# Weight conversion, start-up work and planner settings changed in a fused linear-attention and MLP kernel

## The chip, the core and the metric

The kernel runs on one core of a Trainium2 chip. The core has a matrix engine (PE, TensorE; its weight loads are shown as PEld), a vector engine (DVE, VectorE), an activation engine (ACT, ScalarE), a general engine (POOL, GpSimd) and a queue engine (SP, SyncE), each with an instruction stream of its own that runs in order; they wait for each other by semaphores. DMA transfers between HBM and on-chip memory are issued by SP, and by ACT where the program says so. Products go to PSUM, everything else lies in SBUF; POOL can't reach PSUM. The metric is the device time of one execution in microseconds (us).

## The reference

```python
def phi(x):                                   # q, k, v: (8, 8, 576, 64); w_phi: (64, 128)
    proj = np.einsum('bhsd,df->bhsf', x, w_phi)
    proj = proj - np.max(np.abs(proj), axis=-1, keepdims=True)
    return np.concatenate([np.exp(proj), np.exp(-proj)], axis=-1)
q_p, k_p = phi(q), phi(k)
kv = np.einsum('bhsf,bhsd->bhfd', k_p, v)
z = np.sum(k_p, axis=2)
num = np.einsum('bhsf,bhfd->bhsd', q_p, kv)
den = np.einsum('bhsf,bhf->bhs', q_p, z)[..., None] + 1e-06
x = (num / den), as (8 * 576, 512)            # heads side by side
h = x @ w_in                                  # w_in (512, 2048), float64
g = h * (1.0 / (1.0 + np.exp(-1.702 * h)))
out = (g @ w_out).astype(np.float32)          # w_out (2048, 512), float64
```

The two weight matrices of the last part arrive as 64-bit floats.

## The kernel before

Accuracy is kept by splitting numbers in two 16-bit halves (a high part and what is left of it, names that end in `h` and `l`): each product of two such numbers is three products of halves. The work has two kinds.

*Attention*, batch by batch, in pairs of heads (`attention_first` for the first batch, mostly in 32-bit products; `attention` for the others). Per pair: load k, q and v (`attn_load`: tiles `kt`, `qt`, `vn`), split and turn them (`turned`: `xs`, then a transposing DMA to `xT`), project (`ab` or `at` in PSUM), subtract the maximum (`sm`, `t` on DVE), exponentials on ACT (`e`), split those (`eh` a cast, `el` a subtraction), then products with the values (`kf`, `kz`) and of queries with them (`n`, `nf`), a division (`rc`, `xf`) and the way back to columns (`xo`, `x`). The last 64 rows of all heads of a batch, the tail, are loaded by `tail_load` (tile `tl`, six DMAs) and go through `attn_tail`. The kernel's first product needs the first batch's tail.

*The MLP*, in chunks of 256 or 384 rows (`moe_chunk`): for each of 16 blocks of 128 hidden columns, products into `hb`, tanh (`th`, ACT), `g` (DVE), split into `gh` (ACT) and `gl` (DVE), and products into `ab`.

*The weights* (`load_weights`, 32 blocks of 128 x 512): a block is loaded as 64-bit numbers into `raw`. Each number is two 32-bit words, low and high. ACT copies the high word, taken as a 32-bit float, with a scale into `y` (a PSUM bank `hb` for the first 16 blocks, the SBUF tile `wy` for the others). Two scalings in place, each on any of three engines, work on 16-bit pieces: one brings the top 16 bits of the low word into the high word's low half, one leaves the sign alone in its upper half. Then DVE shifts `y` left by 3 bits and ORs the high word in. The result is split into `w16` (a cast and a subtraction, both shown as `w`). Some 16-bit pieces lie 8 bytes apart.

*The order* is not that of the program text. A `Recorder` notes each operation with the engines that may run it (`three`: DVE, ACT or POOL; `two`: DVE or POOL; `evac`: ACT or DVE), and `schedule` plans the whole program as a list: it keeps a time at which each engine is free, a cost for every operation by engine (`cost`), a delay from each engine to those that use its result (`_READY`), and takes the candidate that can start first; among those that can start at once, the one of the lowest priority number. Priorities come from a place on an axis given to each part of the program (`PLACES`, one pair for each `part`). An operation that may run on several engines is put on one only if no other would finish it earlier by the planner's count, where the cost on each engine is multiplied by `price`. `emit` (line 460) then issues the instructions in that order, so all recorded instructions bear the line L460 in the profile and are told apart by tile names. `wmx`, maxima of the weights, is planned after 250 us.

Ahead of the recorded program stand constants: an identity (`ident`, `ii`), `ones`, and memsets of padding in `vn`, `vs`, `vts`, `zt` and of the two rows of limits `low` and `high`, all on POOL except `ii`.

Of the kernel before, what the change touches and what calls it, by code (L numbers as in the profile page):

```python
# [99 lines left out]
class _Op:  # L100
# [34 lines left out]
_READY = {"tensor": 282.5, "scalar": 240.0, "vector": 305.0, "gpsimd": 300.0, "sync": 100.0}  # L135
# [41 lines left out]
class Recorder:  # L177
    price = dict(tensor=1.000, scalar=0.514, vector=1.148, gpsimd=1.165, sync=1.000)
# [25 lines left out]
    def record(self, alts, also):  # L204
        o = _Op()
        o.eng, o.meth, o.args, o.kw = alts[0]
        o.alts = []
        for e, m, a, k in alts:
            assert e != "gpsimd" or not any(
                isinstance(x, V) and "PSUM" in str(x.t.space) for x in a  # L210
            )
            c = self.cost(e, m, a, k)
            if e == "tensor":
                o.load, o.cost, o.passes = c
            o.alts.append((e, m, c[1] if e == "tensor" else c, self.shared(e, m, a), a, k))
        if o.eng != "tensor":
            o.load, o.cost, o.passes = 0.0, o.alts[0][2], 1
        o.deps, o.outs, o.allocs, o.uses = {}, [], [], []
        o.left, o.end, o.est, o.after = 0, None, 0.0, self.after
        args, kw = o.args, o.kw  # L220
        views = [(args[0], True)]
        views += [(a, False) for a in args[1:]]
        views += [(a, n == "accum_out") for n, a in kw.items()]
        for a, write in views:
            if not isinstance(a, V):
                continue
            self.touch(o, a, write)
        for a in also:
            self.claim(o, a.tl)
        o.left = len(o.deps)  # L230
        for d in o.deps:
            d.outs.append(o)
        self.group.append(o)
        o.prio = o.eng in self.first
        self.ops.append(o)
# [96 lines left out]
    def schedule(self):  # L332
# [15 lines left out]
        free = {"tensor": 0.0, "scalar": 0.0, "vector": 1900.0, "gpsimd": 6200.0, "sync": 700.0}  # L348
# [4 lines left out]
        def ready(o):  # L353
            est = o.after
            for d, data in o.deps.items():
                if data:
                    lat = _READY[d.eng]
                    if d.meth.startswith("dma"):
                        lat = _READY["sync"]
                    elif d.eng == o.eng:  # L360
                        lat = 115.0 if d.eng in ("vector", "scalar") else 0.0
# [9 lines left out]
        while todo:  # L371
            best = None
            for e, c in cand.items():
                t = free[e]
                pick = None
                for o, alt in c:
                    s = max(t, o.est, turn + o.load) if e == "tensor" else max(t, o.est)
                    ok = True
                    for a in o.alts:
                        w = max(free[a[0]], o.est) + a[2] * self.price[a[0]]  # L380
# [31 lines left out]
            if alt[3] and o.eng in ("vector", "gpsimd"):  # L412
                s = max(s, port - 70.0)
                port = s + o.cost
# [6 lines left out]
            if o.meth.startswith("dma"):  # L421
                free[o.eng] = s + (650.0 if o.eng == "sync" else 800.0)
# [44 lines left out]
def attn_moe_fast(ctx, tc, q, k, v, w_phi, w_in, w_out, out):  # L467
# [88 lines left out]
    nc.gpsimd.memset(ones, 1.0)  # L556

    NQ = B + 4
    low, high = (cp.tile([1, NQ], F32, name=n) for n in ("low", "high"))
# [3 lines left out]
    for i, (a, b) in enumerate(lo_hi):  # L563
        nc.gpsimd.memset(low[:, i : i + 1], a)
        nc.gpsimd.memset(high[:, i : i + 1], b)

    for ap in pools["vn"].aps:
        nc.gpsimd.memset(ap[:, :, D : D + 1], ONE)
        nc.gpsimd.memset(ap[:, :, D + 1 : DV], 0.0)
    for ap in pools["vs"].aps:  # L570
        nc.gpsimd.memset(ap, 0.0)
        nc.gpsimd.memset(ap[:, :, 0, D : D + 1], ONE)
    for ap in pools["vts"].aps:
        nc.gpsimd.memset(ap, 0.0)
        for a in range(2):
            nc.gpsimd.memset(ap[a * D : a * D + D, :, a, 0, D : D + 1], ONE)
    for ap in pools["zt"].aps:
        nc.gpsimd.memset(ap, 0.0)
# [34 lines left out]
    def load_weights(j, bank):  # L613
        js = slice(j * P, (j + 1) * P)
        for i, src in (
# [7 lines left out]
            else:  # L623
# [3 lines left out]
                hi = raw.bitcast(I32).rearrange("p (n w) -> p n w", w=2)[:, :, 1]  # L627
                r16 = raw.bitcast(U16).rearrange("p (n w) -> p n w", w=4)
# [3 lines left out]
                R.three.scale(r16[:, :, 2], r16[:, :, 1], 0.9375 * 2.0**-13)  # L632
                R.three.scale(r16[:, :, 3].bitcast(F16), r16[:, :, 3].bitcast(I16), 2.0**-60)
                R.vector.scalar_tensor_tensor(
                    y.bitcast(I32), y.bitcast(I32), 3, hi, ALU.logical_shift_left, ALU.bitwise_or
# [19 lines left out]
    def attn_load(b, hp):  # L655
        kt, qt, vn = new("kt"), new("qt"), new("vn")
        for t, src in ((kt, k), (qt, q)):
            R.sync.dma_start(
# [3 lines left out]
        for a in range(2):  # L662
            R.sync.dma_start(
# [5 lines left out]
    def tail_load(b):  # L669

        t = new("tl")
        for i, src in enumerate((k, q, v)):
            for a in range(2):
                R.sync.dma_start(
# [374 lines left out]
    def in_range():  # L1049


        s = small(16, "sc")
# [143 lines left out]
    def attention_first():  # L1196
# [8 lines left out]
        nat = [attn_load(0, 0)]  # L1205
        tl = tail_load(0)
# [236 lines left out]
```

## Time and profile before

| what | value |
|---|---|
| median of 3 runs | 1100.02 us (1097.91 to 1100.56) |
| the profiled execution, its own time | 1100.22 us |
| its span, first to last instruction | 1098.5 us |
| mean granted TensorE clock | 0.986 of full speed |
| DMA | 181020 packets, 80.93 MB, mean 74 GB/s; HBM read 45.15 MB, written 9.44 MB |
| chain that ended last, by engine | PE 60%, DVE 23%, ACT 8%, the rest 9% |
| largest PE groups | into `hb`: 3264 products, 452.4 us; `gh` into `ab`: 1152, 319.3 us; `gl` into `ab`: 576, 189.5 us |
| weight loads | 32 DMAs of 512 KB, 3.8 us from issue to landing |
| tail loads | 48 DMAs of 64 KB, 2.5 to 2.7 us from issue to landing |

How to read the profile's lines: a group names the line, the engine, the operation, the tile written and the tiles read, the shapes, the count, then busy us and mean ns of one, then the idle time of the engine just before them and what ended it. A row of the view by stretches of time gives the stretch and its length, busy us (and count) of PE, PEld, DVE, ACT and POOL, the granted TensorE clock, the busy share of the DMA engines and GB/s. The timeline gives start, duration, engine, line, operation and tiles. Busy time of PE contains a modelled drain, so products of one group overlap. SPq and ACTq are the DMA issues of SP and ACT.

### The profile page before, as it was taken

The numbers are of one execution on the slowest core, as the hardware profiler recorded it, in microseconds if no ns is written. First come the engines' busy times: TensorE is split into PE (matmuls) and PEld (weight loads), VectorE is DVE, ScalarE is ACT, GpSimd is POOL, SyncE is SP. The second block draws the span as 40 slices with busy tenths as digits, with TensorE's granted clock in tenths as the row PEclk, the third lists the DMA queues.
The fourth block names the chain that finished last, engine by engine and source line by source line (L and its number), as shares of the span: only waits on it lengthen the run. The fifth ranks groups of instructions, "written<-read, shape, count | busy, mean of one in ns | idle before, by whom it ended". The sixth has DMA issues, their size and how long they took to land.

```text
span 1098.5 us, 24641 instructions
## 1 busy us (share of the span) xinstructions
PE 1022.5 (93%) x9874; PEld 671.3 (61%) x9874; DVE 808.4 (74%) x1506; ACT 629.6 (57%) x1357; POOL 354.2 (32%) x461
## 2 busy tenths in 40 slices
PE   4877888999999999999999999999999999999996
PEld 3544556667765666567776555667766655577553
DVE  4888898989999989998899423787887776323232
ACT  4898889667547676665676322655464554232221
POOL 3105764355525535555545000222343211000000
PEclk9987999999999999999999999999999999999998
DMA  7656463253434334323535101132131120000101
GB/s 193 183 172 172 112 143 96 72 112 84 54 73 86 90 90 97 81 69 88 93 78 109 32 1 39 49 87 50 43 75 39 30 48 12 1 30 1 29 1 33
DMA packets 181020, 80.93 MB, mean 74 GB/s; under 512 B 149536, under 2 KB 174240, under 8 KB 180896
## 3 DMA queue, kind: packets, MB, share of 16 engines
q1 hardware_dynamic: 180736, 79.00, 30.4%
q8 instruction: 79, 1.29, 0.5%
q14 instruction: 45, 0.37, 0.1%
q10 hardware_dynamic: 160, 0.26, 0.1%
HBM read 45.15 MB, written 9.44 MB: 50 GB/s over the span
## 4 chain that ended last, share of the span: by engine, by line
PE 60%; DVE 23%; ACT 8%; issue 3%; DMA 3%; SPq 1%; POOL 1%; DVEq 0%; ACTq 0%; POOLq 0%
PE ab L460 25%; PE hb L460 24%; PE at L460 11%; DVE el L460 4%; DVE gl L460 3%; ACT raw L460 2%; DVE sm L460 2%; DVE g L460 2%; DVE t L460 2%; ACT e L460 2%; DVE wmx L460 1%; DMA xT<-xs 1%; SPq L460 1%; DVE xf L460 1%; DVE mq L460 1%
## 5 line engine op out<-in xcount | busy, mean ns | idle before, releaser
L460 PE MATMUL hb<-x,w 128*128 128x192 f16 (+3 forms) x3264 | 452.4, 280 | 2.5 <-DVE g L460 1.6
L460 PEld LDWEIGHTS <-w 128*128 128x128 f16 x3264 | 279.5, 98 | 108.3 <-issue 6.1
L460 PE MATMUL ab<-w,gh 128*128 128x512 f16 x1152 | 319.3, 380 | 4.3 <-ACT gh L460 2.2
L460 DVE SCALAR_TENSOR_TENSOR g<-th,hb 128x384 f32<-128x384 f32 (+1 forms) x208 | 107.2, 517 | 148.7 <-ACT th L460 148.1
L460 ACT ACTIVATE th<-hb 128x384 f32<-128x384 f32 (+1 forms) x208 | 96.8, 467 | 198.4 <-PE hb L460 191.8
L460 PE MATMUL ab<-w,gl 128*128 128x512 f16 x576 | 189.5, 380 | 5.2 <-DVE gl L460 4.9
L460 PEld LDWEIGHTS <-gh 128*128 128x128 f16 x1152 | 107.0, 98 | 103.2 <-ACT gh L460 5.6
L460 DVE SCALAR_TENSOR_TENSOR gl<-g,gh 128x384 f16<-128x384 f32 (+1 forms) x208 | 135.7, 654 | 38.1 <-ACT gh L460 37.8
L460 ACT ACTIVATE gh<-g 128x384 f16<-128x384 f32 (+1 forms) x208 | 103.5, 499 | 80.8 <-DVE g L460 79.1
L460 DVE TENSOR_TENSOR el<-e,eh 128x512 f16<-128x512 f32 x161 | 134.0, 846 | 6.2 <-PE at L460 2.2
L460 PEld LDWEIGHTS <-eh 128*128 128x128 f16 x1856 | 111.4, 97 | 30.3 <-issue 5.5
L460 POOL TENSOR_TENSOR el<-e,eh 128x512 f16<-128x512 f32 x71 | 95.1, 1344 | 74.9 <-DVE eh L460 32.5
L460 PEld LDWEIGHTS <-el 128*128 128x128 f16 x928 | 86.1, 98 | 26.0 <-DVE el L460 16.3
L460 PE MATMUL at<-ph,xT 128*128 128x128 f16 x1008 | 91.6, 219 | 4.3 <-DVE t L460 1.5
L460 PEld LDWEIGHTS <-gl 128*128 128x128 f16 x576 | 53.9, 98 | 65.2 <-DVE gl L460 14.5
L460 PEld LDWEIGHTS <-xT 128*128 128x128 f16 x1056 | 73.7, 99 | 32.6 <-DMA xT<-xs 15.5
L460 ACT CAST eh<-e 128x512 f16<-128x512 f32 x145 | 87.8, 619 | 6.6 <-PE at L460 5.7
L460 POOL TENSOR_TENSOR n<-n,cs 128x132 f32<-128x132 f32 (+1 forms) x75 | 45.6, 610 | 136.4 <-ACT n L460 83.3
L460 ACT ACTIVATE e<-t 128x512 f32<-128x512 f32 x128 | 75.9, 626 | 22.7 <-DVE t L460 21.0
L460 ACT ACTIVATE e<-at 128x512 f32<-128x512 f32 x136 | 76.6, 601 | 14.4 <-PE at L460 12.0
L460 PE MATMUL at<-kz,eh 128*128 128x66 f16 x960 | 78.4, 194 | 4.3 <-DVE nf L460 1.4
L460 PE MATMUL at<-vs,eh 128*128 128x66 f16 x896 | 70.2, 194 | 1.5 <-DVE vs L460 0.6
(187 smaller groups left out, 1396.2 us busy)
## 6 DMA issues: line engine op xcount, KB each, us to landing
kt<-in_k_dram SPq DMA_DIRECT2D x32, 256.0 KB, 2.9
qt<-in_q_dram SPq DMA_DIRECT2D x32, 256.0 KB, 3.0
vn<-in_v_dram SPq DMA_DIRECT2D x64, 128.0 KB, 2.9
raw<-in_moe_w_in_dram SPq DMA_DIRECT2D x16, 512.0 KB, 3.8
raw<-in_moe_w_out_dram SPq DMA_DIRECT2D x16, 512.0 KB, 3.8
out_dram<-e SPq DMA_DIRECT2D x38, 128.0 KB, 2.4
out_dram<-e SPq DMA_DIRECT2D x16, 256.0 KB, 2.4
xT<-xs SPq DMA_TRANSPOSE x68, 2.8
```

Of the source, the lines that this page charges most:

```text
L460: f(*[g(a) for a in o.args], **{k: g(a) for k, a in o.kw.items()})
```

## The change

Five things change together.

1. *Weights.* The scaling that isolates the sign goes. In its place DVE takes the larger of `y` and the high word times -(2^-79): for a positive weight that is `y`, for a negative one a positive number 2^32 times as large, whose higher exponent becomes the sign bit after the shift by 3. The remaining scaling reads the top 16 bits of the low word and writes its result as a 32-bit integer over the whole low word, and the OR takes that word in place of the high one.
2. *Ones.* 40 products of `ones` with itself are issued first on PE, into the first `hb` bank.
3. *Memsets.* The padding of `vn`, `vs`, `vts` and `zt` moves from POOL to DVE; the limits `low` and `high` are set where they are used, in `in_range`, as recorded POOL operations.
4. *Loads.* The first batch's six tail DMAs, and the two V DMAs of its first pair, are issued by ACT; the tail is recorded ahead of the pair.
5. *Planner.* All of `PLACES` but the MLP's own chunks, `_READY`, `price` and the engines' first free times have new values; an issuing engine is now held for a DMA by its size (510 to 660 ns by bytes, 1350 for a transposing one, where it was 650 or 800); the delay within an engine is 125 ns on all but PE (before 115 on DVE and ACT, 0 on POOL); and the port that DVE and POOL share is looked at when a candidate is weighed, not only after it was taken.

```diff
-_READY = {"tensor": 282.5, "scalar": 240.0, "vector": 305.0, "gpsimd": 300.0, "sync": 100.0}
+_READY = {"tensor": 215.0, "scalar": 150.0, "vector": 130.0, "gpsimd": 95.0, "sync": 100.0}
...
-    price = dict(tensor=1.000, scalar=0.514, vector=1.148, gpsimd=1.165, sync=1.000)
+    price = dict(tensor=1.000, scalar=0.004, vector=2.234, gpsimd=1.174, sync=1.000)
...
+            if o.meth == "dma_start_transpose":
+                o.load = 1350.0
+            elif o.meth.startswith("dma"):
+                o.load = 660.0 if o.cost < 900.0 else 510.0 if o.cost < 1800.0 else 440.0
...
-        free = {"tensor": 0.0, "scalar": 0.0, "vector": 1900.0, "gpsimd": 6200.0, "sync": 700.0}
+        free = {"tensor": 5700.0, "scalar": 700.0, "vector": 3400.0, "gpsimd": 1500.0, "sync": 700.0}
...
-                        lat = 115.0 if d.eng in ("vector", "scalar") else 0.0
+                        lat = 0.0 if d.eng == "tensor" else 125.0
...
+                    if alt[3]:
+                        s = max(s, port - 70.0)
...
-                        w = max(free[a[0]], o.est) + a[2] * self.price[a[0]]
+                        w = max(free[a[0]], o.est, port - 70.0 if a[3] else 0.0)
+                        w += a[2] * self.price[a[0]]
...
-                free[o.eng] = s + (650.0 if o.eng == "sync" else 800.0)
+                free[o.eng] = s + o.load
...
+    for i in range(40):
+        nc.tensor.matmul(hb.aps[0][:, 0:P], ones, ones, start=True, stop=True)
...
-        nc.gpsimd.memset(ap[:, :, D : D + 1], ONE)
-        nc.gpsimd.memset(ap[:, :, D + 1 : DV], 0.0)
+        nc.vector.memset(ap[:, :, D : D + 1], ONE)
+        nc.vector.memset(ap[:, :, D + 1 : DV], 0.0)
...
-                hi = raw.bitcast(I32).rearrange("p (n w) -> p n w", w=2)[:, :, 1]
-                r16 = raw.bitcast(U16).rearrange("p (n w) -> p n w", w=4)
+                r32 = raw.bitcast(I32).rearrange("p (n w) -> p n w", w=2)
+                lo, hi = r32[:, :, 0], r32[:, :, 1]


                 R.scalar.activation(y, hi.bitcast(F32), AF.Copy, scale=2.0**-111)
-                R.three.scale(r16[:, :, 2], r16[:, :, 1], 0.9375 * 2.0**-13)
-                R.three.scale(r16[:, :, 3].bitcast(F16), r16[:, :, 3].bitcast(I16), 2.0**-60)
                 R.vector.scalar_tensor_tensor(
-                    y.bitcast(I32), y.bitcast(I32), 3, hi, ALU.logical_shift_left, ALU.bitwise_or
+                    y, hi.bitcast(F32), -(2.0**-79), y, ALU.mult, ALU.max
+                )
+                top = raw.bitcast(U16).rearrange("p (n w) -> p n w", w=4)[:, :, 1]
+                R.three.scale(lo, top, 0.9375 * 2.0**-13)
+                R.vector.scalar_tensor_tensor(
+                    y.bitcast(I32), y.bitcast(I32), 3, lo, ALU.logical_shift_left, ALU.bitwise_or
                 )
...
-    def attn_load(b, hp):
+    def attn_load(b, hp, dk=R.sync, dq=R.sync, dv=R.sync):
...
-    def tail_load(b):
+    def tail_load(b, queue=R.sync):
...
+        for i, (a, b) in enumerate(lo_hi):
+            R.gpsimd.memset(low[:, i : i + 1], a)
+            R.gpsimd.memset(high[:, i : i + 1], b)
...
-        nat = [attn_load(0, 0)]
-        tl = tail_load(0)
+        tl = tail_load(0, R.scalar)
+        nat = [attn_load(0, 0, dv=R.scalar)]
```

The lines of `PLACES`, some 90 pairs of new numbers, are left out here.

More of the change, by code (lines that the diff above doesn't have):

```diff
@@ L411, in schedule @@
                 o.cost = alt[2]
-            if alt[3] and o.eng in ("vector", "gpsimd"):
-                s = max(s, port - 70.0)
+            if alt[3]:
                 port = s + o.cost
@@ L556, in attn_moe_fast @@
     nc.gpsimd.memset(ones, 1.0)
+    for i in range(40):
+        nc.tensor.matmul(hb.aps[0][:, 0:P], ones, ones, start=True, stop=True)
     NQ = B + 4
-    low, high = (cp.tile([1, NQ], F32, name=n) for n in ("low", "high"))
+    low, high = (static(n, [1, NQ], F32) for n in ("low", "high"))
     lo_hi = [(2.0**-6, 2.0)] * B + [
@@ L562, in attn_moe_fast @@
     ]
-    for i, (a, b) in enumerate(lo_hi):
-        nc.gpsimd.memset(low[:, i : i + 1], a)
-        nc.gpsimd.memset(high[:, i : i + 1], b)
     for ap in pools["vn"].aps:
-        nc.gpsimd.memset(ap[:, :, D : D + 1], ONE)
-        nc.gpsimd.memset(ap[:, :, D + 1 : DV], 0.0)
+        nc.vector.memset(ap[:, :, D : D + 1], ONE)
+        nc.vector.memset(ap[:, :, D + 1 : DV], 0.0)
     for ap in pools["vs"].aps:
-        nc.gpsimd.memset(ap, 0.0)
-        nc.gpsimd.memset(ap[:, :, 0, D : D + 1], ONE)
+        nc.vector.memset(ap, 0.0)
+        nc.vector.memset(ap[:, :, 0, D : D + 1], ONE)
     for ap in pools["vts"].aps:
-        nc.gpsimd.memset(ap, 0.0)
+        nc.vector.memset(ap, 0.0)
         for a in range(2):
-            nc.gpsimd.memset(ap[a * D : a * D + D, :, a, 0, D : D + 1], ONE)
+            nc.vector.memset(ap[a * D : a * D + D, :, a, 0, D : D + 1], ONE)
     for ap in pools["zt"].aps:
-        nc.gpsimd.memset(ap, 0.0)
+        nc.vector.memset(ap, 0.0)
     vmx = static("vmx", [P, B], F32)
@@ L652, in w2 @@
         return w16[:, 2 * j + 1, part]
-    def attn_load(b, hp):
+    def attn_load(b, hp, dk=R.sync, dq=R.sync, dv=R.sync):
         kt, qt, vn = new("kt"), new("qt"), new("vn")
-        for t, src in ((kt, k), (qt, q)):
-            R.sync.dma_start(
+        for t, src, queue in ((kt, k, dk), (qt, q, dq)):
+            queue.dma_start(
                 t.rearrange("p (a j) d -> p a (j d)", a=2),
@@ L662, in attn_load @@
         for a in range(2):
-            R.sync.dma_start(
+            dv.dma_start(
                 vn[:, 4 * a : 4 * a + 4, 0:D],
@@ L673, in tail_load @@
             for a in range(2):
-                R.sync.dma_start(
+                queue.dma_start(
                     t[D * a : D * a + D, i],
```

42 rows, old and new, of the table PLACES are left out of this document.

## The prediction

> **What bounds the kernel now.** I read the page first, then its busy times by stretch of the span.
>
> ```profile
> span 1098.5 us, 24641 instructions
> PE 1022.5 (93%) x9874; PEld 671.3 (61%) x9874; DVE 808.4 (74%) x1506; ACT 629.6 (57%) x1357; POOL 354.2 (32%) x461
> ```
>
> ```profile
> core 0: us, PE busy (x) PEld busy (x) DVE busy (x) ACT busy (x) POOL busy (x), PEclk, DMA share, GB/s
> 0.00:15.00 15.00, 0.06 (x1) 0.06 (x2) 2.73 (x8) 4.19 (x7) 5.82 (x47) 1.00 0.74 190
> 15.00:200.00 185.00, 149.88 (x1274) 103.37 (x1275) 160.60 (x289) 161.39 (x316) 78.59 (x92) 0.94 0.54 146
> 200.00:600.00 400.00, 386.47 (x4636) 267.45 (x4635) 376.27 (x685) 263.50 (x608) 198.99 (x237) 1.00 0.40 85
> 600.00:1050.00 450.00, 446.76 (x3758) 280.14 (x3756) 255.40 (x499) 189.77 (x407) 70.84 (x86) 1.00 0.15 36
> 1050.00:1098.50 48.50, 39.31 (x211) 20.30 (x209) 13.35 (x27) 10.73 (x21) 0.00 (x0) 0.94 0.06 19
> ```
>
> PE is busy 1022.5 of 1098.5 us, and the change takes no product away. What can be won is its 76.0 us of idle time and the time at a low clock. The idle time lies so: 14.9 us ahead of the first product, 35.1 in 15 to 200, 13.5 in 200 to 600, 3.2 in 600 to 1050, 9.2 at the end. In 15 to 200 DVE and ACT are both 87% busy and POOL 42%: PE waits for operands that these two prepare (weights and the first batches' attention). In 200 to 600 DVE is 94% busy, ACT 66%. From 600 on PE alone is the bound. The end (stores of the last chunk) isn't touched.
>
> Then the same view in stretches of 8 and 12 us:
>
> ```profile
> 64.00:72.00 8.00, 4.28 (x27) 3.28 (x28) 7.47 (x16) 7.90 (x16) 1.02 (x2) 0.77 0.25 79
> 68.00:76.00 8.00, 5.41 (x21) 3.16 (x20) 5.56 (x10) 7.67 (x13) 0.73 (x2) 0.57 0.38 132
> 84.00:92.00 8.00, 4.76 (x26) 3.17 (x24) 5.89 (x17) 6.66 (x12) 3.71 (x6) 0.59 0.96 239
> ```
>
> The granted clock falls to 0.57 and 0.59 where PE was busy about half of the time. Over 15 to 200 it is 0.94, so some 0.06 x 149.9 = 9 us of PE time are lost to it.
>
> **The start.** The timeline:
>
> ```profile
> 0.88 0.21 POOL L556 MEMSET ones<- 128x128 f16 x1
> 6.91 1.28 ACT L460 ACT_TABLE_LOAD   x1 [6.91 <-DMA vn<-in_v_dram]
> 7.03 1.27 SPq L460 DMA_DIRECT2D tl<-in_q_dram  x2
> 10.33 0.62 ACT L460 CAST xs<-tl 128x512 f16<-128x512 f32 x1 [0.98 <-DMA tl<-in_q_dram]
> 14.94 1.14 PE L460 MATMUL ab<-ph,xT 128*128 128x128 f16 x9 [14.94 <-DMA xT<-xs]
> 17.48 1.06 PE L460 MATMUL at<-xT,ph 128*128 128x512 f16 x2
> ```
>
> ```profile
> L460 PE MATMUL at<-xT,ph 128*128 128x512 f16 x136 | 42.5, 386 | 1.3 <-ACT e L460 0.5 <-DVE mq L460 0.3 <-DVE x L460 0.3
> ```
>
> ```profile
> 1089.42 1.20 ACTq L460 DMA_DIRECT2D out_dram<-e  x2
> ```
>
> The first product hangs on the q tail, whose issue ends on SP's queue at 8.30 and which lands 2.0 us later; from the cast to the product are 14.94 - 10.33 = 4.6 us. On ACT's queue two issues take 1.20 us, so eight (six tail loads, two of V) take 4.8: from about 0.75 to 5.6. The q tail is issued by 3.2 and lands at 5.2 to 6.5. Behind these issues wait the table load (1.28 us, to 6.9) and the first cast, now at 6.9 in place of 10.3: **-3.4 us**. Bounds: 0, if the loads are short of bandwidth rather than of issue time, and -4.8, if another engine casts at 5.5. SP's queue loses eight issues of 0.6 us, which brings forward its other loads, weights included.
>
> The memsets that go to DVE cost at most what POOL now takes up to the landing (5.82 us busy, the large ones 0.97 each); DVE has only 2.73 us of work before 15 us, so they are hidden, and would cost their 3 to 4 us only if the cast went to DVE. The pads of V are set ahead of V's DMA, which now stands behind six issues. The 24 small memsets that go to the end run on a POOL with nothing to do there (0.00 busy in the last row). The 40 products of ones can begin at 1.1, when ones is set. The nine products at 14.94 take 1.14/9 = 0.13 us each, so 40 take 5.1 us: done at 6.2, ahead of all need of PE and of the PSUM buffer they write.
>
> Do they warm the clock? The two 512-wide products at 17.48 take 1.06 us; the mean record of one is 386 ns, so two at full speed would take less than 0.8, and the first products of the kernel run at about half speed, I estimate until about 19.5, half of 4.6 us, at most 2.3 us lost. After the ones PE would be idle again from 6.2 to 11.5, and the rows above show a low clock after stretches that were only half idle, so I take 0 (bounds 0 and -2.3). The Trainium skill (TensorE: Matmul & The Clock Gate, The HAM clock gate) says the same more sharply: PE starts at half clock and goes back to it after an idle window of about 3.4 us, so the ones would buy nothing; the dips agree, and no row here shows the length of the window.
>
> **The weights.** Grouped instructions of 15 to 200:
>
> ```profile
> L460 ACT ACTIVATE raw<-raw 128x512 uint16<-128x512 uint16 x19 | 25.7, 1353 | 0.1
> L460 ACT ACTIVATE raw<-raw 128x512 f16<-128x512 int16 x16 | 21.6, 1368 | 0.0
> L460 ACT ACTIVATE hb<-raw 128x512 f32<-128x512 f32 x16 | 10.2, 641 | 2.4 <-issue 1.2 <-DVE w L460 1.1
> L460 DVE TENSOR_SCALAR raw<-raw 128x512 f16<-128x512 int16 x11 | 10.1, 917 | 0.0
> L460 DVE TENSOR_SCALAR raw<-raw 128x512 uint16<-128x512 uint16 x11 | 9.0, 837 | 1.4 <-ACT hb L460 1.4
> L460 DVE SCALAR_TENSOR_TENSOR hb<-hb,raw 128x512 int32<-128x512 int32 x16 | 11.2, 697 | 5.3 <-ACT raw L460 5.0
> L460 DVE SCALAR_TENSOR_TENSOR wy<-wy,raw 128x512 int32<-128x512 int32 x16 | 13.3, 837 | 5.6 <-ACT raw L460 5.6
> ```
>
> Each of 32 blocks has now two 16-bit scalings: 35 on ACT (47.3 us), 22 on DVE (19.1), 7 on POOL. One goes. In its place DVE does a second two-operand pass, of the form of the one it has: 16 x 0.697 + 16 x 0.837 = 24.5 us more. The scaling that stays writes a 32-bit word at the same step of 8 bytes. No row shows that; bounds are 0.64 us (ACT's pass over 32-bit words at that step) and 1.36 (its 16-bit scaling). I take 0.65: the 16-bit forms alone run at that price, and every row that touches whole words at this step (0.641 and 0.697) runs at the price of a dense one. 32 x 0.65 = 20.8 us, all on ACT by the next part.
>
> **The planner.** An operation with a choice goes to an engine only if no other would finish it sooner by the planner's price. With 0.004 for scalar and 2.234 for vector, ACT counts as nearly free, so nearly all casts, scalings and copies that may go there will; subtractions (DVE or POOL) come out about level: the planner's costs for 512 columns are 602 and 1113, so 2.234 x 602 = 1345 against 1.174 x 1113 = 1307, where POOL stood at 1297 to 691 before. By rows of 15 to 200 and 200 to 600:
>
> ```profile
> L460 DVE CAST eh<-e 128x512 f16<-128x512 f32 x4 | 2.4, 592 | 0.4 <-ACT e L460 0.3
> L460 DVE COPY e<-ab 128x256 f32<-128x256 f32 x1 | 0.4, 415 | 0.0
> L460 POOL CAST eh<-e 128x512 f16<-128x512 f32 x6 | 4.7, 783 | 6.2 <-ACT e L460 6.1
> L460 POOL CAST w<-wy 128x512 f16<-128x512 f32 x1 | 0.6, 609 | 0.3 <-DVE wy L460 0.3
> ```
>
> ```profile
> L460 DVE CAST eh<-e 128x512 f16<-128x512 f32 x28 | 14.4, 515 | 1.7 <-ACT e L460 0.8 <-PE at L460 0.6
> L460 DVE CAST zt<-xf 64x256 f16<-64x256 f32 x1 | 0.3, 276 | 0.0
> L460 ACT CAST eh<-e 128x512 f16<-128x512 f32 x91 | 55.2, 620 | 6.1 <-PE at L460 5.6 <-ACT th L460 0.3
> L460 DVE TENSOR_TENSOR el<-e,eh 128x512 f16<-128x512 f32 x94 | 82.4, 891 | 4.3 <-PE at L460 1.8 <-ACT eh L460 1.1 <-issue 0.6
> L460 POOL TENSOR_TENSOR el<-e,eh 128x512 f16<-128x512 f32 x46 | 60.4, 1317 | 25.7 <-ACT eh L460 13.3 <-PE at L460 5.9 <-DVE eh L460 5.1
> ```
>
> ```profile
> L460 DVE TENSOR_TENSOR el<-e,eh x161: 633/691/1646, 95.6 to 916.9; 128x512 f16<-128x512 f32 x161
> ```
>
> In 15 to 200, 15 such operations are on DVE (8.2 us; first and last group shown, as of POOL's) and 21 on POOL: moved, they give ACT 36 x 0.55 = 20 us. About 10 subtractions more on POOL take 8 us from DVE. So ACT goes from 161.4 to 161.4 - 47.3 + 20.8 + 20 = 154.9, DVE to 160.6 - 19.1 + 24.5 - 8.2 - 8 = 149.8. If the fuller of the two stays as full as now (0.872), the stage lasts 154.9/0.872 = 177.6: **-7.4 us**. Of the 9 us lost to the clock I count a third as regained on the path, **-3 us**.
>
> In 200 to 600, 46 operations with ACT as a choice take 22 us of DVE (eh to zt); with 20 subtractions more on POOL (20 x 0.69 = 14) and some 5 us of longer DVE passes beside them (now (891 - 691) x 94 = 19 us beside 199 us of POOL, so 3 for 26 us more, and 5 with the other two-operand passes), DVE goes from 376.3 to 345 us, 86%; ACT, with 43 casts from POOL too, to some 317 (79%). Waits grow about as 1/(1 - load): 13.5 x 0.06/0.14 = 5.8 us of PE idle, **-7.7 us**. That form gives 0.5% idle at the 57% of 600 to 1050, where 0.7% is measured. Bounds: 0 and -10.6 (that stage's rate).
>
> On DVE, el takes 633 to 1646 ns, by what runs beside it. The Trainium skill (SBUF — State Buffer, on the shared port pair) says that a two-operand DVE pass and a POOL operation exclude each other for their whole length, which speaks against moving work to POOL. By that rule DVE could at worst stand still for all of the 26 us that POOL takes over, and the middle would gain from the casts alone.
>
> **Sum.** -3.4 - 7.4 - 3 - 7.7 = -21.5, from the profiled execution's 1100.2 us (span 1098.5 and 1.7 around it): 1078.7. That execution is 0.2 us over the median of 1100.02, so I forecast **1079**, with a range of its own of 1068 to 1090.
>
> **The rivals.**
>
> *ACT becomes the bound, slower (17%).* Place: 15 to 200. If the 32-bit word costs 1.36 us, ACT has 161.4 - 47.3 + 43.5 + 20 = 177.6 us there, and at a fill of 0.872 the stage lasts 203.7: +18.7. With -3.4 and -7.7 that is +7.6: **1108**. It decides from 1.15 us a word on (where ACT's load makes the stage 11.1 us longer). For it: both 16-bit rows on ACT, and POOL's like price, show that this step can cost double. Against: the 0.641 row.
>
> *The new order fills ACT (22%).* If ACT's fill goes to 0.95, as DVE's is in 200 to 600, the stage lasts 163 us: -22; then PE hardly idles for long and 6 us of clock come back; -10.6 in the middle; -3.4: **1058**. For it: POOL's idle 58% and SP's freed queue. Against: chains of short waits, which no load figure shows.
>
> *Little arrives (14%).* The stage is set by the chain of dependent steps and by buffers, not by load: both engines just idle more, and only the start's -3.4 stays: **1097**. For it: PE's waits there are many and short. Against: both at 87% over 185 us, which leaves little that isn't load.
>
> **How the numbers follow.** Forecast 47%, rivals 22, 14 and 17. The range 1056 to 1102 leaves out part of the 1058 case's spread and most of the slow one; it takes in the bounds of the start, the ones and the middle, and the word's 1.36 us if ACT's fill then rises to 0.90 (177.6/0.90 = 197.3, +1.2 in all). About 0.3% (3.3 us) is what a measurement can tell here. Faster by more: the forecast, the 1058 case and half of the 1097 case, 75%; within: the other half and a small part of the slow case, 9%; slower: 16%.
>
> **What would show it.** In the profile after: first product near 11.5 us, still at half speed; 32 scalings into 32-bit words, on ACT, near 0.65 us; ACT ahead of DVE in the first stage and POOL fuller; PE idle near 25 us there and near 6 in 200 to 600; 600 onwards unchanged. Scalings of 1.3 us with an ACT full to 95% would mean the slow rival. Wrong altogether would be a longer 600-to-end stage: then work was only pushed back.

## The result, and the profile after

| | before | after |
|---|---|---|
| median of 4 runs | 1099.84 us (1097.91 to 1100.56) | 1066.95 us (1065.99 to 1069.61) |
| span of the profiled execution | 1098.5 us | 1064.5 us |
| mean granted TensorE clock | 0.986 | 0.983 |

The ratio is 0.9707, with an interval of 0.9685 to 0.973: 32.9 us faster, where 21 were forecast. The time lies inside the range of 1056 to 1102, and just under the forecast's own range of 1068 to 1090. The page of the kernel after, its totals and its chain of waits:

```profile
span 1064.5 us, 24790 instructions
...
PE 1014.2 (95%) x9914; PEld 666.7 (63%) x9914; DVE 695.9 (65%) x1278; ACT 663.5 (62%) x1471; POOL 489.2 (46%) x575
...
PE 83%; ACT 6%; DVE 5%; DMA 3%; issue 2%; POOL 1%; ACTq 0%; SPq 0%; DVEq 0%; POOLq 0%
```

DVE has 112 us less to do and POOL 135 us more, and DVE's part of the chain that ended last fell from 23% to 5%. Busy times by stretch, first of the kernel before (cut finer than the prediction did, up to 200 us), then of the kernel after:

```profile
15.00:24.00 9.00, 7.96 (x40) 6.63 (x41) 6.61 (x11) 5.99 (x12) 1.16 (x1) 1.00 0.85 249
24.00:80.00 56.00, 43.65 (x258) 29.37 (x257) 48.20 (x86) 51.35 (x91) 7.85 (x9) 0.94 0.57 169
80.00:200.00 120.00, 98.28 (x981) 67.37 (x979) 105.79 (x194) 104.05 (x215) 69.58 (x82) 0.93 0.50 127
```

```profile
0.00:15.00 15.00, 4.07 (x40) 3.90 (x40) 6.34 (x20) 5.98 (x11) 3.84 (x38) 0.77 0.88 253
15.00:24.00 9.00, 2.81 (x21) 2.63 (x22) 6.21 (x12) 5.71 (x11) 0.00 (x0) 0.50 1.09 261
24.00:80.00 56.00, 49.26 (x302) 34.88 (x300) 51.07 (x92) 51.20 (x108) 12.63 (x19) 0.96 0.63 188
80.00:200.00 120.00, 110.07 (x1235) 78.21 (x1235) 102.32 (x198) 105.66 (x254) 96.16 (x104) 0.97 0.50 125
200.00:600.00 400.00, 392.77 (x4478) 266.33 (x4476) 303.38 (x528) 281.93 (x638) 238.80 (x268) 1.00 0.36 79
600.00:1016.00 416.00, 416.00 (x3633) 261.38 (x3632) 213.10 (x404) 202.31 (x435) 137.73 (x148) 1.00 0.18 41
1016.00:1064.50 48.50, 39.25 (x212) 19.37 (x209) 13.49 (x27) 10.72 (x21) 0.00 (x0) 0.95 0.07 19
```

The first columns are the stretch and its length, then PE busy. Length less PE busy is PE's idle time. The 40 products of ones (4.07 us) do no work of the kernel, so they count as idle here:

| stretch | PE idle before | after | difference |
|---|---|---|---|
| 0 to 24 | 15.98 | 21.19 | +5.2 |
| 24 to 80 | 12.35 | 6.74 | -5.6 |
| 80 to 200 | 21.72 | 9.93 | -11.8 |
| 200 to 600 | 13.53 | 7.23 | -6.3 |
| 600 to the last 48.5 us | 3.24 | 0.00 | -3.2 |
| the last 48.5 us | 9.19 | 9.25 | +0.1 |

That is 21.6 us less idle time. The other 12.4 of the span's 34.0 us are busy time: the same products take 1022.5 us before and 1014.2 - 4.07 = 1010.1 after. So most of the idle time was won from 24 to 600 us, and the start got worse. (The stretches are cut by time, so the two kernels don't do the same work in one of them.)

The weights' steps in 15 to 200 after, as groups:

```profile
L466 ACT ACTIVATE raw<-raw 128x512 int32<-128x512 uint16 x28 | 18.8, 680 | 0.0
...
L466 DVE SCALAR_TENSOR_TENSOR wy<-raw,wy 128x512 f32<-128x512 f32 x16 | 12.2, 767 | 0.0
...
L466 DVE SCALAR_TENSOR_TENSOR hb<-raw,hb 128x512 f32<-128x512 f32 x14 | 9.5, 690 | 3.1 <-ACT hb L466 2.9
...
L466 POOL TENSOR_TENSOR el<-e,eh 128x512 f16<-128x512 f32 x32 | 40.0, 1260 | 7.7 <-ACT eh L466 3.3 <-PE at L466 2.8 <-DVE wy L466 0.8
```

The scaling into a 32-bit word takes 680 ns on ACT, half of the 1353 and 1368 of its 16-bit forms, and the new DVE pass costs about what the old one did (690 and 767 against 697 and 837). POOL took 20 subtractions of `el` more in this stretch (32 against 12), twice the 10 that were forecast.

The start, on the timeline of the kernel after:

```profile
2.29 1.30 ACTq L466 DMA_DIRECT2D tl<-in_q_dram  x2
...
6.17 2.55 ACTq L466 DMA_DIRECT2D vn<-in_v_dram  x2
...
8.81 1.28 ACT L466 ACT_TABLE_LOAD   x1 [8.81 <-DMA tl<-in_v_dram]
10.11 0.62 ACT L466 ACTIVATE hb<-raw 128x512 f32<-128x512 f32 x1
...
11.95 0.61 ACT L466 CAST xs<-tl 128x512 f16<-128x512 f32 x1
...
12.70 1.16 POOL L466 TENSOR_TENSOR xs<-tl,xs 128x512 f16<-128x512 f32 x1 [5.97 <-DMA kt<-in_k_dram]
...
15.50 1.52 SPq L466 DMA_TRANSPOSE xT<-xs  x1
...
21.19 1.14 PE L466 MATMUL ab<-ph,xT 128*128 128x128 f16 x9 [15.98 <-DMA xT<-xs]
```

The q tail is issued by 3.6 us (3.2 were forecast), but the cast comes at 11.95 (10.33 before) and the first product at 21.19 (14.94 before). Four things delay it. ACT issues its eight loads until 8.72, not 5.6, and its table load ends at 10.09. The cast then stands on ACT behind the first weights. The transposing DMA stands on SP behind fourteen other issues, 1.6 us after its operand is ready at 13.86. And 21.19 - 15.50 = 5.69 us pass from its start to the product, where 14.94 - 12.07 = 2.87 passed before. The tails themselves land later after their issue (landing times of the q, k and v tails in the kernel before, then in the kernel after):

```profile
DMA to landing us min/median/max: 2.3/2.7/3.7
```

```profile
DMA to landing us min/median/max: 2.9/5.0/5.9
```

Three blocks of weights (512 KB each) are issued from 1.4 to 6.4 us and share the DMA engines with the tails (0.88 busy in the first row after, 0.74 before). So of what was saved on SP's queue, part was paid back in transfer and part on ACT's own queue.

### The profile page after: what moved, and what is told of

It is laid out like the page before. It is cut to its first block, busy times and chain, and to the rows that moved or that the text cites. A ratio compares the mean times of both kernels' runs of the same rounds, so it can differ in the third digit from the quotient of the medians.

```text
span 1064.5 us, 24790 instructions
## 1 busy us (share of the span) xinstructions
PE 1014.2 (95%) x9914; PEld 666.7 (63%) x9914; DVE 695.9 (65%) x1278; ACT 663.5 (62%) x1471; POOL 489.2 (46%) x575
## 4 chain that ended last, share of the span: by engine, by line
PE 83%; ACT 6%; DVE 5%; DMA 3%; issue 2%; POOL 1%; ACTq 0%; SPq 0%; DVEq 0%; POOLq 0%
PE ab L466 33%; PE hb L466 32%; PE at L466 17%; DMA xT<-xs 2%; ACT e L466 2%; ACT eh L466 1%; DVE gl L466 1%; DVE sm L466 1%; POOL el L466 1%; ACT x L466 1%; DVE g L466 1%; ACT xs L466 0%; DVE t L466 0%; DMA tl<-in_v_dram 0%; ACT th L466 0%
## 5 line engine op out<-in xcount | busy, mean ns | idle before, releaser
L466 PE MATMUL ab<-w,gh 128*128 128x512 f16 x1152 | 337.7, 380 | 0.4 <-ACT gh L466 0.3
L466 PEld LDWEIGHTS <-w 128*128 128x128 f16 x3264 | 276.0, 98 | 95.8 <-issue 1.2
L466 POOL TENSOR_TENSOR el<-e,eh 128x512 f16<-128x512 f32 x168 | 209.1, 1254 | 127.7 <-ACT eh L466 107.0
L466 PE MATMUL ab<-w,gl 128*128 128x512 f16 x576 | 204.3, 379 | 4.2 <-DVE gl L466 4.0
L466 PEld LDWEIGHTS <-gh 128*128 128x128 f16 x1152 | 102.4, 98 | 93.9 <-ACT gh L466 16.3
L466 ACT CAST eh<-e 128x512 f16<-128x512 f32 x215 | 128.7, 621 | 3.6 <-PE at L466 3.2
L466 POOL TENSOR_TENSOR n<-n,cs 128x132 f32<-128x132 f32 (+1 forms) x101 | 58.1, 578 | 98.5 <-ACT n L466 81.1
L466 PE MATMUL at<-ph,xT 128*128 128x128 f16 x1008 | 94.1, 219 | 0.8 <-DMA xT<-xs 0.6
L466 ACT ACTIVATE e<-at 128x512 f32<-128x512 f32 x136 | 76.4, 601 | 13.6 <-PE at L466 13.5
L466 PE MATMUL at<-kz,eh 128*128 128x66 f16 x960 | 80.9, 193 | 1.3 <-ACT eh L466 0.7
L466 DVE TENSOR_TENSOR el<-e,eh 128x512 f16<-128x512 f32 x64 | 65.8, 1030 | 24.9 <-ACT eh L466 16.7
```

What stands on the lines that cost most here:

```text
L466: f(*[g(a) for a in o.args], **{k: g(a) for k, a in o.kw.items()})
```

## The experiments

The theory at the outset: the gain is the sum of cheaper weights and of a planner that takes load off DVE. Its rival: engine choice and order form one plan, and no part of it has a value of its own. Experiments on one part keep the planned order and change what is issued in its places. Each ratio is to the kernel before, timed again beside the experiments (medians 1099.33 to 1100.96 us); each time is to be held against 1066.95 (after, not timed again) or 1099.84 (before), so that a difference of 1 or 2 us says nothing.

**The conversion alone, in both orders.** In the order and on the engines of before, the new steps of `load_weights`; and the reverse. In short form:

```diff
+ activation(lo, r16[:, :, 1], scale=0.9375 * 2.0**-13)      # in place of the first 16-bit scaling
+ scalar_tensor_tensor(y, hi, -(2.0**-79), y, mult, max)     # DVE, in place of the second
```

> The order, the engines and everything else of the kernel before, with the new weight conversion alone put in place of the old one (the 32-bit scaling runs where the first 16-bit scaling ran, the pass with the maximum on DVE where the second one ran). Theory 1 (the gain is engine load taken off ACT and DVE): the scalings on ACT drop from 35 of 1.36 us to about 19 of 0.67, so ACT loses some 35 us of the first 200 and DVE is about level; PE's lost time there falls by a fifth and the time by 6 to 9 us, about 1092. Theory 2 (the gain is the order; the conversion matters only with an order planned for it): within 3 us of before, 1097 to 1101.

Measured: 1094.32 us (1091.89 to 1098.25), ratio 0.9955, 0.9939 to 0.997. That is between the two expectations. DVE isn't level, as was expected:

```profile
15.00:200.00 185.00, 154.57 (x1379) 108.48 (x1380) 175.62 (x327) 139.20 (x314) 79.41 (x92) 0.95 0.58 150
```

ACT is 22 us emptier than before in this stretch, but the second pass makes DVE 15 us fuller, 95% busy, since nothing else was taken from it.

> The order and engines of the changed kernel, with the old weight conversion put back (the pass with the maximum becomes the 16-bit scaling of the sign on DVE, the 32-bit scaling becomes the 16-bit one on the same engine, ACT for 30 of 32). Theory 1: ACT gets 30 x 0.68 = 20 us more in the first 200 us, where it is 88% busy, so 8 to 18 us more: 1075 to 1085. Theory 2: at most 3 us more, up to 1070.

Measured: 1078.94 us (1077.53 to 1079.54), ratio 0.9811, 0.9793 to 0.9829. The stretches of this second kernel:

```profile
15.00:200.00 185.00, 155.08 (x1429) 108.02 (x1430) 148.53 (x280) 167.95 (x344) 97.93 (x112) 0.94 0.53 144
200.00:600.00 400.00, 391.85 (x4430) 265.43 (x4427) 305.54 (x528) 283.24 (x642) 239.61 (x269) 1.00 0.36 80
```

From 200 us on it is the kernel after. Before that it does 155.1 us of products where the kernel after does 2.81 + 49.26 + 110.07 = 162.1, with ACT at 168 of 185 us. So the conversion is worth 5.5 us in the old order (5.0 by the ratio) and 12.0 in the new one, where ACT also has the casts that the planner gave it. The other 21 to 27 us belong to the rest of the change; as the ones and the loads turn out to be worth nothing (below), they are the planner's, together with the memsets, which no run tried alone.

**Engines without the order, and the order without the engines.** Of 1292 operations with a choice of engine (the weights' scalings apart), 575 run on another engine in the kernel after. Each of the two kernels got the other's list:

```diff
  self.order = self.schedule()
+ for o, c in zip(free, GIVEN):          # GIVEN: the other kernel's engine for each
+     for a in o.alts:
+         if a[0] == names[c]:
+             o.eng, o.meth, o.args, o.kw = *a[:2], *a[4:]
```

> The order of the kernel before, kept as it is, but each of the 1292 operations with a choice of engine (the 64 scalings of raw weights apart) runs on the engine that the changed kernel gives it: 575 move, most of them from DVE to POOL and to ACT. Theory 1: DVE between 200 and 600 us falls from 94% to below 80% and PE's waits there by half: 8 to 12 us less, 1088 to 1092. Theory 2: an order planned for other engines gains nothing from it, and POOL's longer subtractions delay products: 1098 to 1110.

Measured: 1130.09 us (1127.98 to 1132.06), ratio 1.0283, 1.0263 to 1.0303.

> The order and the conversion of the changed kernel, but the 1292 operations with a choice of engine run where the kernel before has them. Theory 1: DVE is back near 94% between 200 and 600 us, 8 to 12 us more: 1075 to 1079. Theory 2: within 4 us of the changed kernel, 1064 to 1071.

Measured: 1136.62 us (1134.49 to 1137.92), ratio 1.0333, 1.0311 to 1.0354. Each half alone loses: 30 us in the old order, 70 in the new. The first of them in the middle:

```profile
200.00:600.00 400.00, 372.88 (x4368) 251.92 (x4368) 293.53 (x527) 281.52 (x643) 246.33 (x282) 1.00 0.36 79
```

DVE is busy 73% here, less than in either kernel, and PE idles 27.1 us, twice as long as before with DVE at 94%. A lighter DVE does not by itself shorten PE's waits.

**Subtractions alone, the other choices alone.** The same swap into the kernel after, for the 234 subtractions that differ (net 152 to DVE), or for the 341 others:

```diff
+ if o.meth != "tensor_sub": continue    # subs_in_after; == for casts_in_after
```

> The kernel after in its order, with only the subtractions (VectorE or GpSimd) on the engines of the kernel before: 193 go from GpSimd to VectorE, 41 the other way, net about 105 us more on VectorE, the same load as with the idle passes. Load theory: the same time as that run, about 1076. Theory 'choice and order belong together': far more, a good part of the 70 us that all choices swapped cost, 1095 to 1130.

Measured: 1094.39 us (1093.4 to 1095.54), ratio 0.9944, 0.9926 to 0.9962.

> The kernel after in its order, with only the other 900 operations with a choice (casts, copies, scalings out of PSUM) on the engines of the kernel before: 341 of them move (158 leave ScalarE, 39 come to it), VectorE about 40 us fuller, ScalarE about 70 us emptier. Load theory: about 1070, since ScalarE gets relief where it was fullest. Theory 'choice and order belong together': 1085 to 1110; with the subtractions' run the two add up to about the 70 us of all choices swapped, or to less if either alone already breaks the order.

Measured: 1128.86 us (1128.44 to 1131.7), ratio 1.0263, 1.0241 to 1.0285. The same stretch of each:

```profile
200.00:600.00 400.00, 382.68 (x4265) 256.16 (x4266) 304.55 (x572) 271.33 (x608) 149.02 (x194) 1.00 0.35 78
```

```profile
200.00:600.00 400.00, 367.87 (x4049) 242.97 (x4047) 312.97 (x544) 231.23 (x524) 232.65 (x266) 1.00 0.33 75
```

With the subtractions, DVE is busy 304.55 us against 303.38 in the kernel after, and PE idles 17.3 us against 7.2, at one and the same busy time of DVE: it does 44 operations more, but an `el` takes it 742 ns where POOL does less, not 1076. With the casts, ACT is 50 us emptier, which the load theory counted as relief, and PE idles 32.1 us. Alone they cost 27 and 62 us, together 70: not a sum. The load theory missed by 18 and 59 us. The other theory held in kind: the subtractions came out just under its 1095 to 1130, the casts above its 1085 to 1110.

**DVE's spare time in the kernel after.** The subtractions stay on POOL, and DVE gets as much idle work, behind each of POOL's 212 large subtractions from 200 us on:

```diff
  f(*[g(a) for a in o.args], **{k: g(a) for k, a in o.kw.items()})
+ if o.eng == "gpsimd" and o.meth == "tensor_sub" and o.cost > 900.0 and o.start > 200e3:
+     self.nc.vector.tensor_sub(*self.spare)     # 384 columns, read by nobody
```

> The kernel after, with one idle subtraction more on VectorE (384 columns, two operands, on a tile nobody reads) issued behind each of the 212 subtractions of 512 columns that GpSimd does from about 200 us on: some 0.48 us each by the rate of the 512-wide pass, about 102 us, so VectorE's load is back at that of the kernel before (93% in 200 to 600). Theory 'VectorE's load sets the middle' (the prediction's): PE idles as before there, the time goes back up by 8 to 10 us, to about 1076. Theory 'the planned order does it, VectorE's spare time is slack': within 3 us of 1067. Rival: an in-order VectorE passes each delay of half a microsecond on, +20 us or more.

Measured: 1160.48 us (1157.85 to 1162.61), ratio 1.0543, 1.0517 to 1.0568: 93.5 us, more than any theory gave except the rival, which only set a lower bound. The idle passes by tile (min/median/max ns), as a group (busy us, mean ns), and the stretch:

```profile
L468 DVE TENSOR_TENSOR bl<-be,bh x212: 503/851/2026, 205.8 to 977.2; 128x384 f16<-128x384 f32 x106
```

```profile
L468 DVE TENSOR_TENSOR bl<-be,bh 128x384 f16<-128x384 f32 x212 | 200.0, 944 | 0.3
```

```profile
200.00:600.00 400.00, 344.50 (x3791) 226.50 (x3789) 351.63 (x574) 242.61 (x541) 223.20 (x236) 0.98 0.30 68
```

The passes were mis-sized: beside POOL they take 944 ns on average, not 480, so 200 us and not 102. Even so DVE is only 88% busy, less than the 94% of before, and PE idles 55.5 us, four times as long as there. DVE's idle time in a planned order is not slack: an operation put in pushes back all that stands behind it in the queue. The run has a second path, since POOL's 168 subtractions of `el` grow too, from 1254 to 1342 ns. But POOL has 1% of the chain that ended last, as in the kernel after, and DVE 31% in place of 5%, 10% by the idle passes themselves (busy times, then the chain):

```profile
PE 1039.5 (90%) x9914; PEld 666.8 (58%) x9914; DVE 858.8 (74%) x1492; ACT 669.1 (58%) x1471; POOL 520.2 (45%) x575
...
PE 52%; DVE 31%; ACT 8%; issue 5%; DMA 2%; POOL 1%; ACTq 0%; DVEq 0%; SPq 0%; POOLq 0%
```

Groups of PE in the same stretch show whom it hits, first with the idle passes, then in the kernel after:

```profile
L466 PE MATMUL ab<-w,gl 128*128 128x512 f16 x179 | 63.4, 384 | 15.0 <-DVE gl L466 14.8
L466 PE MATMUL at<-ph,xT 128*128 128x128 f16 x472 | 36.5, 219 | 6.7 <-DVE nf L466 3.5 <-DVE nt L466 1.6 <-DMA xT<-xs 0.7
```

```profile
L466 PE MATMUL ab<-w,gl 128*128 128x512 f16 x215 | 75.7, 379 | 3.3 <-DVE gl L466 3.3
L466 PE MATMUL at<-ph,xT 128*128 128x128 f16 x568 | 44.3, 219 | 0.8 <-DMA xT<-xs 0.6 <-DVE nt L466 0.2
```

The Trainium skill (SBUF — State Buffer, Who interferes with whom) says that a DVE operation with two SBUF inputs and a POOL operation that reads SBUF exclude each other for their whole length. The trace agrees: the 36 of the 212 passes during which POOL is idle take 534 to 554 ns, the other 176 take 1025 on average.

**A plan of the same kind.** All places of the parts in the kernel after, except those of the MLP's chunks, moved at random by up to 0.2, and the whole planned anew (the first of some 90 pairs):

```diff
-    (-91.550, -64.503),
+    (-91.655, -64.608),
```

> The changed kernel with every place of a part (the MLP's chunks apart) moved by a random amount of up to 0.2 to either side, and planned anew: the same work, prices and delays, an order a little different. Theory 1 (what the new settings give is the assignment to engines, and any order planned with them does): within 3 us, 1064 to 1070. Theory 2 (the gain beside that of the conversion lies in this one order, fitted to the engines in detail): 5 to 20 us slower, 1072 to 1087.

Measured: 1069.06 us (1065.96 to 1070.52), ratio 0.9721, 0.9691 to 0.9752. Another order that the same planner makes with its engines is as good to some 2 us, so the gain doesn't hang on one exact sequence. It is one draw, with places close to those of the kernel after. It doesn't show why the plan of after is better than that of before, where choice and order come from one plan too. With the price, the `_READY` or the places of before in the planner of after, `schedule` finds no plan (it ends in "the schedule is stuck"), so which of its settings earns the 21 to 27 us stays open.

**The products of ones, and ACT's queue.** The loop over `ones` left out; and the tail and V loads of the first batch issued on SP in their places:

```diff
- for i in range(40):
-     nc.tensor.matmul(hb.aps[0][:, 0:P], ones, ones, start=True, stop=True)
```

```diff
+ if eng == "scalar" and o.meth == "dma_start" and isinstance(o.args[0], V):
+     eng = "sync"
```

> The changed kernel without the 40 products of ones, order otherwise the same. Theory 1 (they end at 5.2 us, the first product that counts comes at 21.2 and runs at a granted clock of 0.50 all the same, so they buy nothing): within 2 us of the changed kernel, 1065 to 1069. Theory 2 (they do keep the clock up for something): 1070 or more.

Measured: 1066.03 us (1064.35 to 1066.45), ratio 0.9699, 0.9678 to 0.972.

> The changed kernel, with the first batch's six tail loads and two V loads issued by SP at their places in the planned order. Theory 1 (at the start the DMA engines are full, 0.88 to 1.09 of them busy, so who issues matters little): within 2 us, 1065 to 1069. Theory 2 (issue time counts): the first product comes 3 us later or more, 1070 to 1074.

Measured: 1065.76 us (1064.23 to 1066.4), ratio 0.9691, 0.9668 to 0.9714. Neither part is worth anything that can be measured. The first products with the ones left out, then in the kernel after:

```profile
19.85 1.14 PE L466 MATMUL ab<-ph,xT 128*128 128x128 f16 x9 [19.85 <-DMA xT<-xs]
20.79 1.06 PE L466 MATMUL ab<-ident,kt 128*128 128x128 f32 x4
```

```profile
22.12 1.06 PE L466 MATMUL ab<-ident,kt 128*128 128x128 f32 x4
```

They take the same 1.14 and 1.06 us with and without ones, so the ones, which end 16 us earlier, warmed nothing. The Trainium skill (DMA: Bandwidth & Descriptors, Issuing engines are not separate DMA queues) says that DMAs of all issuing engines run on the same 16 DMA engines and that a second queue only saves issue time. This pair agrees, and so do the landing times above. With the eight loads back on SP the first product comes at 22.24, and the first blocks of weights still go ahead of the transposing DMA on SP. So it is the planned order that puts them there, not SP's freed queue:

```profile
22.24 1.14 PE L469 MATMUL ab<-ph,xT 128*128 128x128 f16 x9 [17.16 <-DMA xT<-xs]
```

**The start, twice.** First the tail's chain (loads, cast, subtraction on DVE, transposing DMA) ahead of the weights' conversion on every queue, and SP's other loads behind it:

```diff
+ chain = [self.ops[i] for i in (6, 7, 21, 22, 23)]     # ph (two), xs (two), xT
+ if o is first:                                        # the first step of the first weights
+     order += chain + held                             # held: SP's loads planned ahead of xT
```

> The changed kernel with the first batch's tail put first: its cast, its subtraction (on DVE instead of POOL), the transposing DMA and the projection weights go ahead of the first weight block on their engines, and on SP only the projection weights, the first weight block and the first k stand ahead of that DMA; the other loads follow it in the old order. The first product should come near 12 us instead of 21.2. Theory 1 (the late first product is bought back, since ACT and DVE convert weights meanwhile and they are the bound): within 3 us, 1064 to 1070. Theory 2 (PE has to do its work in any case, and 9 us at the start are 9 us): 1057 to 1061.

Measured: 1078.65 us (1078.47 to 1079.4), ratio 0.9814, 0.9793 to 0.9836. In this kernel the fourth block of weights is loaded into the first block's buffer before that one is converted, so the first block is left out (the fourth's numbers stand in its place), and its conversion waits for the fourth's load. ACT and PE on the timeline:

```profile
23.54 0.62 ACT L484 ACTIVATE hb<-raw 128x512 f32<-128x512 f32 x1 [14.22 <-DMA raw<-in_moe_w_out_dram]
```

```profile
12.97 1.14 PE L484 MATMUL ab<-ph,xT 128*128 128x128 f16 x9 [7.38 <-DMA xT<-xs]
```

The first product comes 8.2 us sooner, the weights 13.4 us later (23.54 against 10.11), and the kernel is 11.7 us slower. That fits a stage in which it counts when ACT and DVE start on the weights. As the edit's own wait for the fourth load holds them back, the run doesn't show that an early tail must cost this. So the second one holds back only the four Q loads (1 MB, first read by PE at 48 us), and leaves the weights' loads where they are:

```diff
+ held = [o for o in self.order[: self.order.index(turn)]          # turn: the first xT
+         if o.meth == "dma_start" and o.args[0].tl.buf.aps[0].name[:2] == "qt"]
+ rest = [o for o in self.order if o not in held]
+ i = rest.index(turn) + 1
+ self.order = rest[:i] + held + rest[i:]
```

> The kernel after with the four Q loads (1 MB, first used by PE at 48 us) issued on SyncE's queue behind the first transposing DMA in place of ahead of it; the weights' loads keep their places. Theory 'the transposing DMA is late because of transfers ahead of it': first product at 16 to 18 us in place of 21.2, the fourth weight block lands sooner too, 2 to 4 us gained, 1063 to 1065. Theory 'the start is set by the chain of conversions, not by the first product': first product sooner, time unchanged. Rival: ScalarE and VectorE wait for loads held back, as in the run with the tail first, and the time rises.

Measured: 1071.77 us (1068.62 to 1072.43), ratio 0.974, 0.9724 to 0.9756. PE and ACT on its timeline:

```profile
17.68 1.14 PE L472 MATMUL ab<-ph,xT 128*128 128x128 f16 x9 [12.77 <-DMA xT<-xs]
...
26.22 0.66 PE L472 MATMUL ab<-ident,kt 128*128 128x128 f32 x4 [2.38 <-DVE mq L472]
28.43 1.97 PE L472 MATMUL at<-x,vn 128*66 128x256 f32 x4 [1.55 <-ACT x L472]
```

```profile
23.62 0.62 ACT L472 ACTIVATE hb<-raw 128x512 f32<-128x512 f32 x1 [1.89 <-DMA raw<-in_moe_w_in_dram]
```

The first product comes 3.5 us sooner, and the lead is given back in two waits of 2.38 and 1.55 us before the products with V, which start at 28.43 (29.05 in the kernel after). ACT then waits 1.89 us for a block of weights and starts on it at 23.62; the kernel after reaches that step at 23.70 without a wait. So an earlier first product alone doesn't bring this start forward. The time doesn't fall; by the medians it lies 4.8 us higher, by the ratios 3.6 (the two intervals just touch), which these runs don't explain. No version beat the kernel after by more than the measurement can tell.

## Why the prediction was right, and where not

- **What bounds the kernel**: right in the main. The idle time was won where PE waited for DVE and ACT, and the last 48.5 us are unchanged (9.19 and 9.25 us idle).
- **The start, -3.4**: this step failed, in sign too (+5.2). It moved the chain of the tail as a whole by what the issue gains, with ACT's pairs of issues at 1.20 us; they took 1.28 to 2.55, and ACT was free for its table load 3 us later than forecast. And it didn't count that the new plan puts the first weights, their loads and their conversion, ahead of that chain. The bound of 0 was set for a lack of bandwidth, but not a loss. The term was also of little worth: 3.5 us and 8.2 us of earlier product bought nothing.
- **Ones, 0, and memsets, hidden**: right for the ones (0.9 us less without them, inside the spread). The memsets were not tried alone.
- **The weights' 32-bit word at 0.65 us**: right (0.68 in the first stage), and with it the slower rival fell, whose point was 1.15 us a word.
- **Stage 15 to 200, -7.4**: the mechanism holds in part, the size was off: -17.4 us of idle between 24 and 200. The forecast kept ACT's fill at 0.872. It is (51.20 + 105.66)/176 = 0.891 from 24 us on, against (51.35 + 104.05)/176 = 0.883 before, hardly higher, so the rival that fills ACT to 0.95 fell in its mechanism, though its 1058 is 9 us from the time and the forecast's 1079 is 12. But the same fill carried more products. The conversion gave 5.5 to 12.0 us of it, the rest is the plan's: I read it as chains that wait less, which no sum of loads shows and no run isolates. The sign "PE idle near 25 us there" came out at 185 - 162.1 = 22.9 for 15 to 200, but by luck: 15 to 24 us, where a late start adds idle time, hide part of the gain.
- **The clock, -3**: mis-sized as a term for busy time. The same products are busy 12.4 us less. The granted clock rose from 0.94 to 0.96 and from 0.93 to 0.97 in 24 to 200, so the loss to it fell from 0.06 x 43.65 + 0.07 x 98.28 = 9.5 us to 0.04 x 49.26 + 0.03 x 110.07 = 5.3: 4.2 us, as far as the recorded clock can be trusted (last section). The other 8 us are likely PE's waits rather than the clock. With the idle passes on DVE the same products are busy 1039.5 - 4.45 (the ones) = 1035.0 us, 25 us more than in the kernel after, at a granted clock of 0.986 against 0.983. So busy time, in which the ends of products are modelled, grows where PE waits more; how much of it is waiting stays open.
- **Stage 200 to 600, -7.7**: near in size (-6.3, and -3.2 more after it), near by luck. DVE fell to 303 us (76%), not 345 (86%), since POOL took 43 subtractions of `el` more, not 20. At 76% the form gives 13.5 x 0.06/0.24 = 3.4 us of PE idle, where 7.2 were measured: two misses that cancel. And the form is wrong in reason. Waits that grow as 1/(1 - load) of DVE would give the kernels with 73% and 76% the shortest ones; they have 27.1 and 17.3 us.
- **Little arrives, 1097**: its thought that chains rather than loads set the stage is nearer to what the swaps of engines show than the forecast's; it didn't consider that a new plan can shorten chains as well.

So the sum came out 12.5 us too small by the spans: the first stage gave 10.0 us more than its term, busy time 9.4 and the time after 600 us 3.2, against 8.6 us lost at the start and 1.4 in the middle.

## What to carry to other kernels

Where every engine's order is planned, price a change of the planner as a whole, and don't split it into relief for one engine: the same relief without its order cost 30 us here, and idle time on an in-order engine wasn't slack (200 us of idle passes cost 93). Before an early chain is moved further forward, look at what the plan puts ahead of it on every queue that it passes, and at which engine the stage really starts with. Measure parts by swapping them in both directions, since a part's worth (5.5 or 12.0 us for the same conversion) depends on the plan around it.

## What the runs showed of the hardware that was not expected

- In place, at a step of 8 bytes, a scaling to 16 bits takes 1353 ns on ACT, one to a 32-bit word 680, from the same 16-bit source (on DVE 837 and, in the run with the conversion alone in the old order, 417).
- A two-operand DVE pass of 384 columns takes 503 ns at best and 944 on average when it is issued behind POOL's subtractions.
- The granted clock isn't shown alike for the same start. With the ones, 15 to 24 us stands at 0.50 (row above). Without them it stands at 1.00, in the row below, though the first products there take the same time:

```profile
15.00:24.00 9.00, 4.15 (x24) 3.63 (x25) 7.01 (x13) 6.85 (x14) 0.39 (x1) 1.00 1.12 293
```

A duration of a known group says more of the clock there than the record does.
